# Retention and two feed-forward layers: q scaled inside its transposes, low parts of the early weights on GpSimd, and smaller conversion steps

## Chip, core and metric

One core of a Trainium2 chip runs the whole program. The metric is the device time of one execution in microseconds (us), the median over runs. The engines work from their own lists of instructions in order: TensorE (PE; its weight loads are PEld), VectorE (DVE), ScalarE (ACT), GpSimd (POOL) and SyncE (SP), which here only issues transfers. They wait for each other by semaphores.

## What is computed

Retention over four sequences of 576 tokens with 8 heads of 64, and behind it two feed-forward layers over the 2304 tokens:

```python
gamma = 1.0 - 2.0 ** (-5.0 - np.arange(H, dtype=np.float32))
rel = pos[:, None] - pos[None, :]
Dmat = np.where(rel >= 0, gamma[:, None, None] ** rel[None, :, :], 0.0)
attn = ((q @ k.T) / np.sqrt(64) * Dmat) @ v            # for each sequence and head
x = attn with its heads side by side                   # 2304 x 512
h = np.maximum(np.maximum(x @ w1, x @ w2), x @ w3)     # 2304 x 768
x2 = h @ w_out                                         # 2304 x 512
g = x2 @ w_gate
out = (g / (1 + np.exp(-g)) * (x2 @ w_val)) @ w_out2   # 2304 x 512, inner width 1536
```

The weights arrive in 64-bit form.

## The kernel before

**Units and visits.** The retention is cut into 32 units n: a sequence, a half of it (288 tokens, three chunks of 96) and a pair of heads. `visit(n)` loads unit n+4 (`a_load`), finishes unit n (`a_value`), computes the states and the scores of unit n+1 (`a_state`, `a_score`), prepares unit n+2 (`a_prep`), and between these does `slices` pieces of the first feed-forward layer (`f_slice`) and `convs` conversions of its weights. Visit 0 has neither, visits 1 and 2 one conversion, visits 3 to 7 one slice and one conversion, visits 8 to 12 five slices and three conversions. In visits 0 to 3 three products with zeros (`spin`) keep TensorE busy. Up to visit 12 every engine's order is the order of the code; from visit 13 only TensorE's is, and a scheduler sets the others.

**A unit's chain.** For units 0 to 15 `a_prep` transposes k and q on TensorE into PSUM (tp); ScalarE copies k's part (kt) and VectorE multiplies q's part by the decay g (qg). For units 16 to 31 VectorE transposes both. GpSimd scales k into ks. `a_state` multiplies ks and v into m_ps, VectorE adds that to the running state (st), and ScalarE spreads the state into stz. `a_score` multiplies kt and qg into s, and VectorE applies the decay mask (pT). `a_value` multiplies stz by qg and v by pT into o_ps; ScalarE makes the high part xh and VectorE the rest xl.

**A slice** is twelve products of a 128 x 128 piece of a weight's high or low part with xh or xl, into one of two PSUM buffers; ScalarE (first of three weights) or VectorE (the other two, hmax) empties it.

**A conversion** of one weight piece from 64 bits (`conv_steps`) is wz and wl on ScalarE, shift, or and add on VectorE, the high part (wh) on ScalarE and the low part (wlo) on the engine given, here VectorE. `win_phase` takes one step; `win_conv(i)` takes ScalarE's first step of weight i+1 beside the high part of weight i, then VectorE's step of i+1, then the low part of i. Weights 3, 4, 8, 9 and so on (i % 5 > 2) lie in tiles w64e, the others in w64; five are in flight.

**The later stages** (second matrix of the first layer, second layer) are not touched.

## Time and profile before

| | us |
|---|---|
| median of 3 runs | 886.98 (885.99 to 888.44) |
| the profiled execution | 885.56 |
| its span, first to last instruction | 883.8 |
| TensorE busy | 861.6 (97%) |
| VectorE busy | 411.4 (47%) |
| ScalarE busy | 278.9 (32%) |
| GpSimd busy | 140.8 (16%) |

The first value product of visit 1 starts at 16.82 us, of visit 8 at 53.77, of visit 13 at 109.89. These times cut the span into the stretches used below. In a row of the windows stand the stretch, its length, then for each engine its busy time and (xN) its instructions, then TensorE's granted clock as a share of 2.4 GHz, the busy share of the DMA engines and GB/s. In a row of the timeline stand start, duration, engine, line, operation, output<-inputs and, in brackets, the engine's idle time just before and what ended it. In rows by line and form stand count, busy us, mean ns and idle time before. A row of the chain has start, duration, engine, output, line and count.

### The profile page before, as it was taken

The page shows a single profiled execution, that of the slowest core. Times are in us where ns is not written, and L with a number is a line of the kernel's source. Part 1 is how long each engine was busy: PE and PEld are TensorE (multiplying, and loading weights), DVE is VectorE, ACT ScalarE, POOL GpSimd, SP SyncE. Part 2 cuts the span into 40 slices and gives each one's busy share as a digit, 9 for nine tenths or more (in the row PEclk, how much of TensorE's full clock was granted, in tenths as well). Part 3 has the DMA queues.
Part 4 walks back from the last instruction along what each step waited for, and adds up shares of the span by engine and source line. Part 5 has one row for each costly group of instructions (what it writes and reads, how often), then busy time and mean ns, then how long its engine had stood idle before and what let it go on. Part 6 is the DMA issues. An engine that isn't in the chain of part 4 may idle for free.

```text
span 883.8 us, 14602 instructions
## 1 busy us (share of the span) xinstructions
PE 861.6 (97%) x5924; PEld 754.9 (85%) x5924; DVE 411.4 (47%) x770; ACT 278.9 (32%) x576; POOL 140.8 (16%) x148
## 2 busy tenths in 40 slices
PE   8889999999999899999999999999999999999998
PEld 5678999999999899999888888888888888888886
DVE  3888844435333962112811642573383353323243
ACT  3656612111113741443732711341151131111111
POOL 2110000001000300543111111121111111111111
PEclk9999999999999999999999999999999999999999
DMA  8866765433201850331400300130030000000122
GB/s 212 196 183 171 215 135 101 92 82 76 60 28 50 258 164 28 92 97 55 143 1 0 120 24 1 48 96 1 1 122 21 1 1 1 1 0 1 48 90 77
DMA packets 128179, 68.34 MB, mean 77 GB/s; under 512 B 89488, under 2 KB 123408, under 8 KB 128112
## 3 DMA queue, kind: packets, MB, share of 16 engines
q1 hardware_dynamic: 127248, 66.78, 28.1%
q8 instruction: 46, 0.75, 0.3%
q10 hardware_dynamic: 864, 0.64, 0.3%
q14 instruction: 21, 0.17, 0.1%
HBM read 55.60 MB, written 11.80 MB: 76 GB/s over the span
## 4 chain that ended last, share of the span: by engine, by line
PE 81%; DMA 6%; DVE 5%; ACT 3%; issue 2%; POOL 1%; SPq 1%; POOLq 0%; DVEq 0%; ACTq 0%
PE ps L503 33%; PE ps L313 19%; PE ps L525 16%; PE ps L478 8%; DMA hf<-h_d 2%; PE s L213 2%; PE o_ps L254 1%; PE o_ps L257 1%; DMA h_d<-hmax 1%; DMA w<-in_moe_w_dram 1%; DVE wz L112 1%; DVE wl L113 1%; PE m_ps L229 1%; ACT wz L108 1%; POOL hl L453 1%
## 5 line engine op out<-in xcount | busy, mean ns | idle before, releaser
L313 PE MATMUL ps<-xl,wh 128*128 128x288 f32 x576 | 175.6, 305 | 8.0 <-DVE hmax L319 4.1
L503 PE MATMUL ps<-x2l,wrh 128*128 128x512 f32 (+1 forms) x480 | 179.4, 374 | 0.7 <-DVE sg L511 0.7
L503 PE MATMUL ps<-x2h,wrl 128*128 128x512 f32 (+1 forms) x480 | 179.2, 373 | 0.0
L503 PE MATMUL ps<-x2h,wrh 128*128 128x512 f32 (+1 forms) x480 | 179.1, 373 | 0.0
L313 PE MATMUL ps<-xh,wh 128*128 128x288 f32 x576 | 170.3, 296 | 0.0
L313 PE MATMUL ps<-xh,wlo 128*128 128x288 f32 x576 | 170.3, 296 | 0.0
L514 POOL TENSOR_TENSOR gl<-gf,gh 128x512 fp32r<-128x512 f32 (+1 forms) x60 | 75.2, 1253 | 388.8 <-ACT gh L513 388.8
L313 PEld LDWEIGHTS ps<-xl,wh 128*128 128x128 f32 x576 | 108.6, 189 | 14.2 <-DVE hmax L319 6.7
L511 DVE TENSOR_TENSOR sg<-ps,sg 128x512 f32<-128x512 f32 (+1 forms) x60 | 38.2, 636 | 170.8 <-ACT sg L510 170.7
L313 PEld LDWEIGHTS ps<-xh,wlo 128*128 128x128 f32 x576 | 108.9, 189 | 0.0
L313 PEld LDWEIGHTS ps<-xh,wh 128*128 128x128 f32 x576 | 108.8, 189 | 0.0
L503 PEld LDWEIGHTS ps<-x2l,wrh 128*128 128x128 f32 x480 | 90.4, 188 | 19.6 <-DVE sg L511 1.6
L503 PEld LDWEIGHTS ps<-x2h,wrl 128*128 128x128 f32 x480 | 90.4, 188 | 17.8
L503 PEld LDWEIGHTS ps<-x2h,wrh 128*128 128x128 f32 x480 | 90.5, 189 | 17.6
L525 PE MATMUL ps<-wrh,gl 128*128 128x512 f32 x216 | 85.8, 397 | 0.4 <-POOL gl L514 0.4
L525 PE MATMUL ps<-wrl,gh 128*128 128x512 f32 x216 | 85.6, 396 | 0.0
L510 ACT ACTIVATE sg<-ps 128x512 f32<-128x512 f32 (+1 forms) x60 | 33.2, 554 | 165.7 <-PE ps L503 165.7
L525 PE MATMUL ps<-wrh,gh 128*128 128x512 f32 x216 | 85.2, 394 | 0.0
L319 DVE TENSOR_TENSOR hmax<-ps,hmax 128x288 f32<-128x288 f32 x96 | 43.4, 453 | 84.4 <-PE ps L313 76.0
L513 ACT ACTIVATE gh<-gf 128x512 fp32r<-128x512 f32 (+1 forms) x60 | 35.2, 587 | 121.1 <-DVE gf L512 121.1
L512 DVE TENSOR_TENSOR gf<-ps,sg 128x512 f32<-128x512 f32 (+1 forms) x60 | 38.2, 636 | 65.4 <-PE ps L503 64.5
L531 DVE TENSOR_TENSOR acc<-ps,acc 128x512 f32<-128x512 f32 x90 | 61.8, 689 | 3.3 <-PE ps L525 2.7
(61 smaller groups left out, 1139.8 us busy)
## 6 DMA issues: line engine op xcount, KB each, us to landing
w<-in_moe_w_out_dram SPq DMA_DIRECT2D x18, 512.0 KB, 3.8
h_d<-hmax SPq DMA_DIRECT2D x48, 144.0 KB, 1.8
hf<-h_d SPq DMA_DIRECT2D x48, 144.0 KB, 2.3
w<-in_moe_w_dram SPq DMA_DIRECT2D x12, 512.0 KB, 4.6
w<-in_moe_w_gate_dram SPq DMA_DIRECT2D x12, 512.0 KB, 4.6
w<-in_moe_w_val_dram SPq DMA_DIRECT2D x12, 512.0 KB, 4.4
kn<-in_k_dram SPq DMA_DIRECT2D x64, 72.0 KB, 2.9
out_dram<-acc SPq DMA_DIRECT2D x18, 256.0 KB, 2.0
```

The lines of the kernel that those rows point to most:

```text
L213: pe.matmul(s[:, e, cs], u["kt"][hd, cs], u["qg"][hd, c], start=True, stop=True)
L313: pe.matmul(ps, l[:, ksl], r, start=n == 0, stop=n == 3 * KD - 1)
L319: dve.tensor_tensor(mx[hb], ps, mx[hb], ALU.max)
L478: pe.matmul(ps, l[:, es], r, start=n == 0, stop=n == 3 * F1 - 1)
L503: pe.matmul(ps[:, 0:tw], l[:, ksl], r, start=n == 0, stop=n == 3 * KD - 1)
L510: act.activation(sg[:, 0:tw], pr[0][:, 0:tw], ACTF.Sigmoid)
L511: dve.tensor_tensor(sg[:, 0:tw], pr[0][:, 0:tw], sg[:, 0:tw], ALU.mult)
L512: dve.tensor_tensor(gf[:, 0:tw], pr[1][:, 0:tw], sg[:, 0:tw], ALU.mult)
L513: act.activation(gh[:, 0:tw], gf[:, 0:tw], ACTF.Copy)
L514: pool.tensor_tensor(gl[:, 0:tw], gf[:, 0:tw], f(gh[:, 0:tw]), ALU.subtract)
L525: pe.matmul(ps, l[:, sl], r, start=n == 0, stop=n == 3 * GRP - 1)
L531: dve.tensor_tensor(a, ps, a, ALU.add)
```

## The change

- **q.** New constants q_t hold g to the power j for each head; GpSimd multiplies them once with the identity into eight diagonal tiles `dia` of 96 x 96. For units 0 to 15 q is no longer transposed: for each chunk and head, q (96 x 64) is the stationary operand and `dia` moves, so transposing and scaling are one product, six per unit in place of three transposes. ScalarE copies k's and q's part together (kq, 576 columns); VectorE's qg is gone there. For units 16 to 31 only buffers change (kq has 3, qt 1).
- **Low parts.** The 18 weights of the first layer have wlo on GpSimd.
- **Steps.** `conv_steps` stops in more places, and `conv_plan` takes, per weight i: shift and or of i, then wz of i+1; add of i, then wl of i+1; high part, then low part of i. The load of weight i+4 goes with the add of i.
- **Order.** xl of unit n now stands behind st of unit n+1 (`low`). For unit 0 the scores precede the states. `zero` is filled before the other tiles.
- **First loads.** cst_a and q0 go on ScalarE's queue, k0 and v0 on SyncE's, cst_g behind weight 1; weights 2 and 3 are loaded in visits 1 and 2.

```diff
+O_Q = O_E + NP
+O_G = O_Q + H
...
+            c[:CK, O_Q + 2 * pr + e] = g ** j
...
+    dia = att.tile([CK, H, CK], F32, name="dia", tag="dia", bufs=1)
...
         z = stg.tile([P, 512], U32, name="wz", tag="wz", bufs=2)
+        act.activation(f(z), f(u[:, :, 1]), ACTF.Copy, scale=float(2.0 ** -112))
+        yield
         l = stg.tile([P, 512], U32, name="wl", tag="wl", bufs=2)
-        act.activation(f(z), f(u[:, :, 1]), ACTF.Copy, scale=float(2.0 ** -112))
         act.activation(l, u[:, :, 0], ACTF.Copy, scale=float(2.0 ** -29))
         yield
         dve.tensor_scalar(z, z, 3, None, ALU.logical_shift_left)
         dve.scalar_tensor_tensor(z, u[:, :, 1], 0x80000000, z, ALU.bitwise_and, ALU.bitwise_or)
+        yield
         dve.tensor_tensor(l, z, l, ALU.add)
...
+    zero = att.tile([P, 512], BF16, name="zero", tag="zero", bufs=1)
+    pool.memset(zero, 0.0)
     stz = [att.tile([P, NC, 2, D], F32, name=f"stz{i}", tag=f"stz{i}", bufs=1) for i in range(3)]
...
-        kt = att.tile([P, C], F32, name="kt", tag="kt", bufs=2)
-        qg = att.tile([P, NC, CK], F32, name="qg", tag="qg", bufs=3)
+        kq = att.tile([P, 2, C], F32, name="kq", tag="kq", bufs=3)
+        kt, qg = kq[:, 0], kq[:, 1].rearrange("p (c m) -> p c m", c=NC)
...
-            for x, nm in ((0, "k"), (1, "q")):
-                for c in range(NC):
-                    pe.transpose(tp[:, x, c * CK:(c + 1) * CK],
-                                 u[nm][:, c].rearrange("p h d -> p (h d)"), ident)
-            act.activation(kt, tp[:, 0, 0:C], ACTF.Copy)
-            dve.tensor_tensor(qg, tp[:, 1, 0:C].rearrange("p (c m) -> p c m", c=NC), g, ALU.mult)
+            for c in range(NC):
+                pe.transpose(tp[:, 0, c * CK:(c + 1) * CK], u["k"][:, c].rearrange("p h d -> p (h d)"), ident)
+            for c in range(NC):
+                for e in range(2):
+                    pe.matmul(tp[64 * e:64 * e + 64, 1, c * CK:(c + 1) * CK], u["q"][:, c, e],
+                              dia[:, 2 * pr + e], start=True, stop=True)
+            act.activation(kq, tp[:, :, 0:C], ACTF.Copy)
         else:
-            qt = att.tile([P, C], F32, name="qt", tag="qt", bufs=2)
+            qt = att.tile([P, C], F32, name="qt", tag="qt", bufs=1)
...
-        dve.tensor_tensor(xl, o, f(xh), ALU.subtract)
         xs[(2 * b + h, pr)] = (xh, xl)
+        return lambda: dve.tensor_tensor(xl, o, f(xh), ALU.subtract)
...
-        win_step[i] = conv_steps(win_ld[i], hi, lo, dve)
+        win_step[i] = conv_steps(win_ld[i], hi, lo, pool)
...
             if phase == 3:
+                win_load(i + 4)
+            if phase == 5:
                 ready.add(i)
-    def win_conv(i, part=None):
-
-        for p, (j, ph) in enumerate(((i + 1, 0), (i, 2), (i + 1, 1), (i, 3))):
-            if part is None or p in part:
-                win_phase(j, ph)
-        if part is None or 3 in part:
-            win_load(i + 4)
+    wc = [0]
+
+    def conv_plan(convs):
+
+        for _ in range(convs):
+            i = wc[0]
+            if i < len(win_units):
+                wc[0] += 1
+                yield (i, 2), (i + 1, 0)
+                yield (i, 3), (i + 1, 1)
+                yield (i, 4), (i, 5)
...
-        a_value(n)
+        low = a_value(n)
...
         a_state(n + 1)
+        low()
         a_score(n + 1)
...
+        for j in range(slices + 1):
+            if j == min(2, slices - 1) or not slices:
                 a_prep(n + 2)
...
+            upto = -(-len(plan) * (j + 1) // (slices + 1))
+            for step in plan[done:upto]:
+                for i, ph in step:
+                    win_phase(i, ph)
+            done = upto
+            if j < slices:
+                f_some(1)
...
-    sp.dma_start(out=cst_a, in_=consts[:, 0:O_G])
-    a_load(0, "kq")
-    act.dma_start(out=cst_g, in_=consts[:, O_G:O_D])
-    a_load(0, "v", act)
+    act.dma_start(out=cst_a, in_=consts[:, 0:O_G])
+    a_load(0, "k")
+    a_load(0, "q", act)
+    a_load(0, "v")
+    pool.tensor_tensor(dia, ident.unsqueeze(1).to_broadcast([CK, H, CK]),
+                       q_t.unsqueeze(2).to_broadcast([CK, H, CK]), ALU.mult)
     act.dma_start(out=cst_d, in_=consts[0:CK, O_D:NCONST])
...
     win_load(1)
-    win_load(2)
-    win_load(3)
+    sp.dma_start(out=cst_g, in_=consts[:, O_G:O_D])
     spin(8)
     a_prep(0)
     spin(3)
+    a_score(0)
     a_state(0)
-    a_score(0)
...
+        if 1 <= n < 3:
+            win_load(n + 1)
```

VectorE, one visit's worth of work around visit 5, before. wz, wl and wlo are a weight's parts, w64e its 64-bit form:

```order
L195 TENSOR_TENSOR qg<-tp,cst_g 128x288
L111 TENSOR_SCALAR wz<-wz 128x512
L112 SCALAR_TENSOR_TENSOR wz<-w64e,wz 128x512
L113 ISA wl<-wz,wl 128x1024
L319 TENSOR_TENSOR hmax<-ps,hmax 128x288
L117 TENSOR_TENSOR wlo<-wl,wh 128x512
L261 TENSOR_TENSOR xl<-o_ps,xh 128x288
L239 SCALAR_TENSOR_TENSOR st<-st,cst_a,m_ps 128x64 x2
L215 TENSOR_TENSOR pT<-s,cst_d 96x576
```

And the same with the change:

```order
L116 TENSOR_SCALAR wz<-wz 128x512
L117 SCALAR_TENSOR_TENSOR wz<-w64e,wz 128x512
L119 ISA wl<-wz,wl 128x1024
L334 TENSOR_TENSOR hmax<-ps,hmax 128x288
L248 SCALAR_TENSOR_TENSOR st<-st,cst_a,m_ps 128x64 x2
L271 TENSOR_TENSOR xl<-o_ps,xh 128x288
L224 TENSOR_TENSOR pT<-s,cst_d 96x576
```

qg and wlo are gone, and st stands ahead of xl.

ScalarE, from the end of unit 8 on (visit 8), before:

```order
L260 ACTIVATE xh<-o_ps 128x288
L243 ACTIVATE stz_83<-st 64x3x64 x2
L108 ACTIVATE wz<-w64e 128x512
L109 ACTIVATE wl<-w64e 128x512
L115 ACTIVATE wh<-wl 128x512
L317 ACTIVATE hmax<-ps 128x288
L194 ACTIVATE kt<-tp 128x288
```

And with the change:

```order
L269 ACTIVATE xh<-o_ps 128x288
L252 ACTIVATE stz_86<-st 64x3x64 x2
L111 ACTIVATE wz<-w64e 128x512
L114 ACTIVATE wl<-w64e 128x512
L332 ACTIVATE hmax<-ps 128x288
L121 ACTIVATE wh<-wl 128x512
L204 ACTIVATE kq<-tp 128x576
```

hmax stands ahead of wh, and the copy of k's part has become the copy of both.

TensorE, the retention part of visit 6, before:

```order
L254 MATMUL o_ps<-qg,stz_83 64x96 x6
L257 MATMUL o_ps<-pT,vn 64x96 x6
L229 MATMUL m_ps<-vn,ks 64x64 x4
L213 MATMUL s<-qg,kt 96x96 x6
L192 MATMUL tp<-cst_a,kn 128x96 x3
L192 MATMUL tp<-cst_a,qn 128x96 x3
```

And with the change:

```order
L263 MATMUL o_ps<-kq,stz_86 64x96 x6
L266 MATMUL o_ps<-pT,vn 64x96 x6
L238 MATMUL m_ps<-vn,ks 64x64 x4
L222 MATMUL s<-kq 96x96 x6
L199 MATMUL tp<-cst_a,kn 128x96 x3
L202 MATMUL tp<-dia,qn 64x96 x6
```

The three transposes of q have become six products in the same place.

## Rows read from the trace of the kernel before

**Rows 1.** Windows: stretch, length, PE, PEld, DVE, ACT, POOL busy, clock, DMA share, GB/s.

```profile
16.82:53.77 36.95, 31.71 (x420) 26.31 (x419) 30.89 (x64) 21.91 (x53) 5.45 (x8) 1.00 0.85 209
...
53.77:109.89 56.12, 52.16 (x510) 49.05 (x510) 48.95 (x96) 34.12 (x71) 3.94 (x6) 0.97 0.70 191
...
60.00:65.00 5.00, 3.01 (x15) 2.90 (x16) 4.21 (x8) 3.94 (x8) 0.82 (x1) 0.79 0.50 133
65.00:70.00 5.00, 4.50 (x39) 4.10 (x39) 4.03 (x8) 2.11 (x5) 0.00 (x0) 0.87 0.44 134
...
109.89:140.00 30.11, 29.38 (x302) 27.77 (x302) 13.83 (x34) 5.96 (x18) 2.83 (x4) 1.00 0.67 134
```

**Rows 2.** Waits of TensorE to 110 us: total, times, longest.

```profile
PE o_ps L254 <- ACT stz L243: 3.6, 5, 1.5
PE ps L313 <- ACT hmax L317: 2.5, 2, 2.0
PE psz L337 <- POOL zero L332: 2.4, 1, 2.4
...
PE tp L192 <- DMA kn<-in_k_dram: 1.4, 2, 1.2
PE tp L192 <- DMA qn<-in_q_dram: 1.0, 1, 1.0
```

**Rows 3.** Timeline of VectorE from one qg to the next; TensorE's m_ps of visit 5.

```profile
37.50 0.46 DVE L195 TENSOR_TENSOR qg<-tp,cst_g 128x288 f32<-128x288 f32 x1 [0.58 <-ACT kt L194]
...
40.49 0.68 DVE L117 TENSOR_TENSOR wlo<-wl,wh 128x512 fp32r<-128x512 f32 x1
...
41.45 0.59 DVE L239 SCALAR_TENSOR_TENSOR st<-st,cst_a,m_ps 128x64 f32<-128x64 f32 x2
41.95 0.75 DVE L215 TENSOR_TENSOR pT<-s,cst_d 96x576 f32<-96x576 f32 x1
43.29 0.46 DVE L195 TENSOR_TENSOR qg<-tp,cst_g 128x288 f32<-128x288 f32 x1 [0.58 <-ACT kt L194]
...
38.08 0.44 PE L229 MATMUL m_ps<-vn,ks 96*64 96x64 f32 x6
```

**Rows 4.** Timeline of ScalarE and TensorE in visit 8.

```profile
59.14 0.73 ACT L243 ACTIVATE stz<-st 64x192 f32<-64x192 f32 x2 [2.55 <-DVE st L239]
...
61.54 0.39 ACT L317 ACTIVATE hmax<-ps 128x288 f32<-128x288 f32 x1
...
61.99 0.40 PE L313 MATMUL ps<-xl,wh 128*128 128x288 f32 x1 [2.00 <-ACT hmax L317]
```

**Rows 5.** Groups by line and form: GpSimd's and ScalarE's prices.

```profile
L514 POOL TENSOR_TENSOR gl<-gf,gh 128x512 fp32r<-128x512 f32 x48 | 64.4, 1343 | 325.9 <-ACT gh L513 325.9
...
L184 POOL TENSOR_TENSOR ks<-kn,cst_a 96x384 f32<-96x384 f32 x16 | 13.6, 852 | 114.1 <-PE m_ps L229 66.9 <-DMA kn<-in_k_dram 47.2
...
L510 ACT ACTIVATE sg<-ps 128x512 f32<-128x512 f32 x48 | 28.7, 599 | 153.5 <-PE ps L503 153.5
```

**Rows 6.** The chain that ended last, early: products of the retention part.

```profile
12.65 0.50 PE tp L192 x6
...
14.06 0.50 PE o_ps L257 x12
...
14.91 0.68 PE s L213 x12
```

**Rows 7.** GpSimd beside VectorE: timeline, and means by form, 12 to 130 us.

```profile
41.72 0.82 POOL L184 TENSOR_TENSOR ks<-kn,cst_a 96x384 f32<-96x384 f32 x1 [3.54 <-DMA kn<-in_k_dram]
...
61.02 0.82 POOL L184 TENSOR_TENSOR ks<-kn,cst_a 96x384 f32<-96x384 f32 x1 [3.33 <-DMA kn<-in_k_dram]
61.05 1.34 DVE L112 SCALAR_TENSOR_TENSOR wz<-w64e,wz 128x512 uint32<-128x512 uint32 x1
...
L215 DVE TENSOR_TENSOR pT<-s,cst_d 96x576 f32<-96x576 f32 x16 | 12.0, 747 | 0.3 <-PE s L213 0.3
...
L112 DVE SCALAR_TENSOR_TENSOR wz<-w,wz 128x512 uint32<-128x512 uint32 x16 | 11.0, 690 | 0.4
```

More of the change, by code (lines that the diff above doesn't have):

```diff
@@ L39 @@
 O_E = O_KS + NP * 2
-O_G = O_E + NP
+O_Q = O_E + NP
+O_G = O_Q + H
 O_D = O_G + NP * CK
@@ L87, in retention_moe @@
     ks_t = cst_a[0:CK, O_KS:O_E].rearrange("p (r e) -> p r e", r=NP)
-    e_t = cst_a[:, O_E:O_G]
+    e_t = cst_a[:, O_E:O_Q]
+    q_t = cst_a[0:CK, O_Q:O_G]
     g_t = cst_g.rearrange("p (r m) -> p r m", r=NP)
     d_t = cst_d.rearrange("p (r e m) -> p r e m", r=NP, e=2)
+    dia = att.tile([CK, H, CK], F32, name="dia", tag="dia", bufs=1)
     def load_w(src, early=False):
@@ L328, in f_some @@
                 f_slice(*fq.pop(0))
-    zero = att.tile([P, 512], BF16, name="zero", tag="zero", bufs=1)
-    pool.memset(zero, 0.0)
     def spin(n):
@@ L339, in visit @@
     def visit(n, slices, convs):
-        nonlocal wc
         a_load(n + 4)
-        a_value(n)
+        low = a_value(n)
         if n == 2 * NP - 1:
@@ L353, in visit @@
         a_state(n + 1)
+        low()
         a_score(n + 1)
-        plan = [p for _ in range(convs) for p in ((0, 1), (2,), (3,))]
+        plan = list(conv_plan(convs))
         done = 0
-        def some(upto):
-            nonlocal done, wc
-            while done < min(upto, len(plan)):
-                if wc < len(win_units):
-                    win_conv(wc, plan[done])
-                if 3 in plan[done]:
-                    wc += 1
-                done += 1
-        for j in range(slices):
-            if j == 2 or slices < 3 and j == 0:
-                a_prep(n + 2)
-            some(-(-len(plan) * (j + 1) // (slices + 1)))
-            f_some(1)
-        if not slices:
-            a_prep(n + 2)
-        some(len(plan))
-    wc = 0
+        for j in range(slices + 1):
+            if j == min(2, slices - 1) or not slices:
+                a_prep(n + 2)
+            upto = -(-len(plan) * (j + 1) // (slices + 1))
[5 more added lines that the diff above has]
+                f_some(1)
     START = 13
```

## The prediction

> **What bounds the kernel now.** I began with the windows, one row per stretch between visits' first value matmuls. From 140 us on TensorE is the bound: already from 109.89 to 140 it is busy 29.38 of 30.11 us [rows 1]. Its list of instructions hardly changes, so what it waits for early is what can be won, and what is added to it is what can be lost. From 16.82 us (visit 1) to 53.77 (visit 8) it is busy 31.71 of 36.95 us: 5.24 lost. From 53.77 to 109.89 (visits 8 to 12) it is busy 52.16 of 56.12: 3.96 lost. After that 0.73 more is lost by 140.
>
> Then the waits: up to 110 us TensorE waited mostly for ScalarE's stz (3.6), for ScalarE's hmax (2.5) and for two loads of k (1.4) [rows 2]. ScalarE is not the cause. In the timeline of visits 4 and 5, VectorE's rows from one qg to the next show one gap, 0.58 us, before qg itself, which waits for ScalarE's kt [rows 3]. The last products m_ps of visit 5 start on TensorE at 38.08 and take 0.44, and VectorE takes up the st that reads them at 41.45: it runs 2.9 us late. stz follows st, and the next visit starts with stz. At 59.14 ScalarE starts an stz for which it had stood 2.55 us behind VectorE; hmax, four instructions later in its order, starts at 61.54, and that ends TensorE's longest wait, 2.0 us [rows 2, 4].
>
> That hole costs twice. After it the granted clock is 0.79 in 60 to 65 us and 0.87 in 65 to 70 [rows 1], which is time at the lower of two levels (1.2 GHz, 0.5): (0.21 + 0.13) x 5 = 1.70 us is lost by it.
>
> So up to 110 us the chain goes through VectorE: 30.89 us busy of 36.95, then 48.95 of 56.12.
>
> **The change, part by part.** *qg leaves VectorE in units 0 to 15.* One qg is 0.46 us [rows 3]; its place is taken by ScalarE, whose copy grows from 288 to 576 columns. 512 columns out of PSUM take 0.60 [rows 5]; scaled, 0.67 for 576. ScalarE is busy 21.91 and 34.12 us of the two stretches, so the growth lies in its free time, and kq is read a visit later. If that cover fails, stz waits behind it, some 0.3 us a visit.
>
> *The low part leaves VectorE*: 18 x 0.68 [rows 3]. On GpSimd 512 columns of the same operation take 1.34 in the last stage, 384 of ks 0.85 [rows 5]: I take 1.34, the same form. GpSimd is busy 5.45 of 36.95 us, so it has room; TensorE uses a weight a visit later or more. ks stands behind the low part in GpSimd's order and is wanted a visit later.
>
> *VectorE's sum.* Visits 1 to 7: 30.89 - 7 x 0.46 - 7 x 0.68 = 22.9 us. Visits 8 to 12, with the 11 remaining weights: 48.95 - 5 x 0.46 - 11 x 0.68 = 39.2. TensorE's own work is 31.71 and 52.16. So TensorE is last in both stretches, unless GpSimd takes it back (below). st also goes ahead of xl, which helps stz; and shift and or now come a step after ScalarE's wz, so their wait for it goes.
>
> *The q products, on TensorE.* Three transposes become six products per unit. The row of six transposes is 0.50, so q's three are 0.25. The products have 96 rows, 64 columns of weights and 96 columns moving, and write two halves in turn: that is the form of the second part of a_value, 0.50 for its six. The scores, six too, take 0.68 [rows 6]. So a unit gains 0.25 us (ends: 0, if a product cost what half a transpose costs, and 0.43). I take 0.25, the same form. Seven fall into visits 1 to 7: 1.75. Five into visits 8 to 12: 1.25. One later.
>
> *The start.* TensorE waits 2.4 us for zero, 0.2 of the 1.4 for the first k, and 1.0 for q0 [rows 2]. zero is now filled first, cst_a and cst_g leave the path of k0, and q0 goes on ScalarE's queue. All of it gone is 1.2 (what zero gains only brings the spins forward). Against it: the diagonal tiles (768 columns, twice the 0.85 of ks, so 1.7) go ahead of q0's products and of the first ks on GpSimd, and the first products run at the lower clock. Between -1.2 and +1.5; I take -0.3, since the diagonal needs only cst_a, which is now ScalarE's first load.
>
> *The queues.* Weights 2 and 3 and cst_g no longer stand ahead of unit 4's loads on SyncE's queue, for whose k TensorE waited 1.2. Weight 3 now goes behind weight 4. Nothing else passes anything that it must wait for.
>
> *The sum.* Visits 1 to 7: -5.24 of waits + 1.75 of products, and 0.9 for waits that stay (a sixth, for bunching), gives -2.6. Visits 8 to 12: -3.96 - 1.70 of clock + 1.25 + 1.6 that stay (weights come there three a visit, so more bunches), gives -2.8. Later: -0.73 + 0.25 + 0.28, -0.2. Start: -0.3. Together -5.9. The profiled execution took 885.56 us (span 883.8), so 879.7; it stands 1.42 below the median of the runs, 886.98, so **881.1**.
>
> **What speaks against it.** At 61.02 GpSimd starts a ks of 0.82 us, and the VectorE instruction of 61.05 takes 1.34 us, where the same operation on the other staging tiles takes 0.69: as if it had begun only at 61.70, just before GpSimd ended. At 41.72 a ks overlaps pT, which reads its products from PSUM, and pT takes 0.75, the mean of its 16 rows [rows 3, 7]. The Trainium skill has this as a rule (SBUF — State Buffer, section "Who interferes with whom"): VectorE instructions with two SBUF inputs, or in a mode that uses two ports, and GpSimd instructions that read SBUF shut each other out for the whole of an instruction. Both pairs of rows agree with it. By that rule the low part, put on GpSimd, is not off VectorE at all; what that gives is the first rival.
>
> **The rivals.**
> (A) *GpSimd's low parts hold VectorE up* (slower). Each low part of 1.34 us falls on shift, or or add. VectorE then has 22.9 + 7 x 1.34 = 32.3 and 39.2 + 11 x 1.34 = 53.9 us; with the holes that it has today (6.06 and 7.17) the stretches take 38.4 and 61.1, against 36.95 and 56.12: +6.4, and 885.56 - 0.3 + 6.4 + 1.42 = 893. It decides from about 1.0 us lost per low part, the 0.68 saved plus qg's share (12 x 0.46 / 18 = 0.31). For it: the row at 61.05. Against: the low part comes after hi, which comes after the add of the same weight; VectorE's next work is then hmax, st, xl and pT, all with an operand in PSUM, as pT at 41.95. With three weights a visit it will hit sometimes; that is in the 1.6.
> (B) *Loads pace visits 1 to 7* (no difference). One visit moves 432 KB of k, q, v and one weight of 512 KB, near 0.97 MB; at the 209 GB/s of the stretch [rows 1] that is 4.6 us. Visits shortened to 34.4/7 = 4.9 leave almost nothing. If loads pace, the first stretch gains nothing and the late weights take half of the second: 885.56 - 1.4 + 1.42 = 885.6. Against: DMA is busy 0.85 there, so it has some reserve.
> (C) *The wait moves to ScalarE* (no difference). hmax stays in order behind two steps of conversion and now kq; if TensorE's buffers wait for it as at 61.54, the clock falls again, and the second stretch only loses products: 885.56 - 2.6 - 0.3 + 1.25 + 1.42 = 885.3. Against: ScalarE is busy 34.12 of 56.12 us there [rows 1].
>
> **How the numbers follow.** Forecast 0.72, A 0.08, B 0.12, C 0.08. 0.3% (2.7 us) is about what a measurement of this kernel can tell from no change; so faster ends at 884.3. The forecast's own range goes from all waits gone with the start at its best, 885.56 - 1.2 - 5.24 - 5.66 - 0.73 + 3.25 + 1.42 = 877.4, a little lower for cheaper products, to the scores' price (13 x 0.18 = 2.3) and more bunching, some 884.5. I set 876.5 to 886.5: B and C are in, A is out. Faster 0.70 (0.02 of the forecast's cases are too small), same 0.20 (B, C), slower 0.10 (A, and a dear start).
>
> **What would show it.** Right: from visit 1 to visit 8 some 34.4 us in place of 36.95, from visit 8 to visit 13 some 53.3 in place of 56.12, no stretch at the lower clock after 15 us, stz started by st soon after m_ps, six q products in about 0.50. Wrong: VectorE's shift, or and add longer than 0.45 and 0.70 beside GpSimd's low part (A); waits of wz or ks for their loads, with DMA over 1.0 (B); waits of TensorE for ScalarE's hmax (C); q products near 0.68.

## The result, and the profile after

The changed kernel takes **879.09 us** (876.93 to 880.24, 4 runs) against 886.54 of before beside it; the ratio is 0.9906 (95% interval 0.9887 to 0.9925), so 0.9% faster. Run again it took 878.36 (876.77 to 881.25, 6 runs; 0.9903, 0.9882 to 0.9923). Forecast were 881.1 us and a range of 876.5 to 886.5. The profiled execution took 880.24 us, span 878.4; against the span of before, 883.8, it is 5.4 shorter, where the sum of the prediction had 5.9. That this agrees is partly luck, as the stretches show (starts of visits as in [rows 1]):

| stretch | before | after | difference | forecast |
|---|---|---|---|---|
| to visit 0 / to visit 1 | 13.51 / 16.82 | 10.67 / 14.47 | -2.84 / -2.35 | -0.3 |
| visit 1 to visit 8 | 36.95 | 33.92 | -3.03 | -2.6 |
| visit 8 to visit 13 | 56.12 | 51.43 | -4.69 | -2.8 |
| visit 13 to the end | 773.91 | 778.58 | +4.67 | -0.2 |

The windows of the changed kernel (columns as in [rows 1]) answer to the first two rows of that group. TensorE is busy 33.48 of 33.92 us and then 51.43 of 51.43; VectorE has gone from 30.89 to 24.69 and from 48.95 to 44.20. Then two stretches with a lower clock stand where before had 1.00:

```profile
14.47:48.39 33.92, 33.48 (x483) 27.76 (x482) 24.69 (x51) 25.19 (x56) 13.42 (x13) 1.00 0.89 225
48.39:99.82 51.43, 51.43 (x557) 48.72 (x557) 44.20 (x75) 32.67 (x66) 22.48 (x18) 1.00 0.74 206
100.00:105.00 5.00, 3.49 (x23) 3.31 (x20) 3.35 (x6) 1.50 (x3) 0.91 (x1) 0.72 0.80 136
105.00:110.00 5.00, 5.00 (x53) 4.50 (x51) 1.47 (x4) 0.82 (x2) 0.00 (x0) 0.94 0.57 125
280.00:300.00 20.00, 18.04 (x120) 17.47 (x121) 18.15 (x32) 14.43 (x28) 6.68 (x7) 0.91 0.84 248
```

TensorE's waits over the whole span (total, times, longest) answer to [rows 2]. The 3.6 us for stz, the 1.4 for k and the 1.0 for q are no longer among them; what is left for hmax waits mostly for VectorE, and late (at 102 and 289 us). The wait for k isn't gone for good: in the second profile (from the run again) TensorE waits 1.4 us for k, and visits 1 to 7 take 34.87 us in place of 33.92.

```profile
PE ps L328 <- DVE hmax L334: 3.4, 2, 1.9
...
...
PE ps L328 <- ACT hmax L332: 0.8, 1, 0.8
```

The timeline shows where both waits for VectorE's hmax stand. On VectorE an add that belongs to w_out, which the scheduler put in early, takes 1.31 us beside a ks of GpSimd; hmax comes behind it, and TensorE has stood 1.51 us. The second hole is at 288.74, again in front of hmax.

```profile
100.10 0.91 POOL L192 TENSOR_TENSOR ks<-kn,cst_a 96x384 f32<-96x384 f32 x1 [1.88 <-PE tp L202]
100.25 1.31 DVE L119 CUSTOM_DVE_ANT_0 wl<-wz,wl 128x1024 uint16<-128x1024 uint16 x1
101.49 0.44 DVE L334 TENSOR_TENSOR hmax<-ps,hmax 128x288 f32<-128x288 f32 x1
...
101.99 0.43 PE L328 MATMUL ps<-xl,wh 128*128 128x288 f32 x1 [1.51 <-DVE hmax L334]
...
288.74 0.40 PE L328 MATMUL ps<-xl,wh 128*128 128x288 f32 x1 [1.86 <-DVE hmax L334]
```

The holes are 1.51 and 1.86 us; the clock costs (0.28 + 0.06) x 5 = 1.7 and 0.09 x 20 = 1.8. The holes alone are not what is new. From visit 13 on all waits of TensorE come to 7.0 us, in before to 5.4; between 270 and 340 us it is idle for 2.95 in the one and 3.03 in the other. So of the 4.67 us in the table's last row some 1.5 are waits and some 3.5 the lower clock, which before has nowhere in that stretch (1.00). The second profile of the same kernel has both holes too (1.57 and 1.94), with the clock at 1.00 behind the first and 0.91 around the second.

What GpSimd's low part, and the ks that now runs behind it, do to VectorE is seen in groups by line up to 110 us (busy, mean ns). On GpSimd the low part takes 1355 ns, as priced. On VectorE the add takes 830 (747 before), shift 596 (424), or 773 [rows 7: 690]:

```profile
L119 DVE CUSTOM_DVE_ANT_0 wl<-wz,wl 128x1024 uint16<-128x1024 uint16 x20 | 16.5, 830 | 2.2
L116 DVE TENSOR_SCALAR wz<-wz 128x512 uint32<-128x512 uint32 x22 | 13.1, 596 | 1.4 <-ACT wz L111 1.4
L117 DVE SCALAR_TENSOR_TENSOR wz<-w,wz 128x512 uint32<-128x512 uint32 x16 | 12.4, 773 | 0.5
...
L123 POOL TENSOR_TENSOR wlo<-wl,wh 128x512 fp32r<-128x512 f32 x18 | 24.4, 1355 | 47.6 <-ACT wh L121 47.6
```

With or on the tiles w64e (1037 after, 848 before, 6 of them) the growth is 20 x 0.083 + 22 x 0.172 + 16 x 0.083 + 6 x 0.189 = 7.9 us, 0.44 per low part. The timeline shows on which instructions it falls. St and xl, which read PSUM, keep their 0.60 (two) and 0.45 beside a low part; a shift that meets one takes 1.04 in place of 0.42, as if it began near the end of the low part (96.24). The low part can be held up as well: the one at 66.11, with an or that began at 66.10, takes 1.84 in place of 1.29, and the add behind that or takes 1.57 in place of 0.69. Of the 18 low parts ten meet only work that reads PSUM, among them all six that fall into visits 1 to 7; eight meet a shift, an or or an add.

```profile
66.10 0.69 DVE L117 SCALAR_TENSOR_TENSOR wz<-w,wz 128x512 uint32<-128x512 uint32 x1
66.11 1.84 POOL L123 TENSOR_TENSOR wlo<-wl,wh 128x512 fp32r<-128x512 f32 x1 [3.34 <-ACT wh L121]
...
66.93 1.57 DVE L119 CUSTOM_DVE_ANT_0 wl<-wz,wl 128x1024 uint16<-128x1024 uint16 x1
...
85.02 1.29 POOL L123 TENSOR_TENSOR wlo<-wl,wh 128x512 fp32r<-128x512 f32 x1 [2.58 <-ACT wh L121]
85.39 0.60 DVE L248 SCALAR_TENSOR_TENSOR st<-st,cst_a,m_ps 128x64 f32<-128x64 f32 x2 [0.74 <-ACT st L246]
85.90 0.45 DVE L271 TENSOR_TENSOR xl<-o_ps,xh 128x288 fp32r<-128x288 f32 x1
...
94.96 1.28 POOL L123 TENSOR_TENSOR wlo<-wl,wh 128x512 fp32r<-128x512 f32 x1 [2.58 <-ACT wh L121]
...
95.48 1.04 DVE L116 TENSOR_SCALAR wz<-wz 128x512 uint32<-128x512 uint32 x1 [0.29 <-ACT wz L111]
```

### The profile page after: what moved, and what is told of

Read it like the earlier page. It is cut to its first block, busy times and chain, and to the rows that moved or that the text cites. A ratio compares the mean times of both kernels' runs of the same rounds, so it can differ in the third digit from the quotient of the medians.

```text
span 878.4 us, 14871 instructions
## 1 busy us (share of the span) xinstructions
PE 865.7 (99%) x6068; PEld 759.3 (86%) x6068; DVE 401.3 (46%) x736; ACT 282.8 (32%) x576; POOL 167.8 (19%) x167
## 4 chain that ended last, share of the span: by engine, by line
PE 86%; DMA 5%; DVE 3%; ACT 2%; issue 2%; POOL 1%; SPq 1%; ACTq 0%; POOLq 0%; DVEq 0%
PE ps L510 33%; PE ps L328 22%; PE ps L532 16%; PE ps L485 7%; DMA hf<-h_d 2%; PE s L222 2%; PE o_ps L263 2%; PE o_ps L266 1%; POOL hl L460 1%; PE m_ps L238 1%; DMA w<-in_moe_w_dram 1%; PE tp L202 1%; DVE wz L117 1%; SPq L161 1%; DVE wz L116 1%
## 5 line engine op out<-in xcount | busy, mean ns | idle before, releaser
L460 POOL TENSOR_TENSOR hl<-hf,hh 128x288 fp32r<-128x288 f32 x48 | 39.4, 840 | 127.8 <-ACT hh L459 126.9
```

The lines of the kernel that those rows point to most:

```text
L460: pool.tensor_tensor(hl, hf, f(hh), ALU.subtract)
```

## The experiments

Medians and ratios are each against before run beside it (886.7, 888.0 and 886.9 us in the three sets).

| kernel | us | ratio, 95% interval |
|---|---|---|
| changed kernel, and again | 879.09, 878.36 | 0.9906 (0.9887-0.9925), 0.9903 (0.9882-0.9923) |
| e1 old loads | 882.19 | 0.9945 (0.9925-0.9965) |
| e2 zero late | 883.00 | 0.9957 (0.9939-0.9976) |
| e14 zero late, two spins | 878.21 | 0.9900 (0.9878-0.9923) |
| e3 low part on VectorE | 882.06 | 0.9948 (0.9928-0.9969) |
| e5 old steps | 888.37 | 1.0013 (0.9999-1.0026) |
| e13 old steps, low part on VectorE | 883.84 | 0.9965 (0.9950-0.9979) |
| e7 before, low part on GpSimd | 892.42 | 1.0062 (1.0040-1.0084) |
| e4 q transposed | 880.01 | 0.9926 (0.9908-0.9944) |
| e9 hmax first | 880.33 | 0.9921 (0.9903-0.9938) |
| e8 order to 16 | 881.40 | 0.9927 (0.9901-0.9953) |
| e12 w_out late | 879.88 | 0.9919 (0.9900-0.9938) |

**The low part and the steps: e3, e7, e5, e13.** My theory was that VectorE had been relieved by the low part; the rival was A, that GpSimd takes it back. In e3 only the engine goes back:

```diff
-        win_step[i] = conv_steps(win_ld[i], hi, lo, pool)
+        win_step[i] = conv_steps(win_ld[i], hi, lo, dve)
```

> The changed kernel with the 18 low parts on VectorE again, all else as it is. They took 0.685 us each there and 1.355 on GpSimd, beside which shift, or and add on VectorE were longer by 7.9 us in all, 0.44 per low part. Theory: VectorE only gets 0.685 - 0.44 = 0.25 us per weight more to do, 1.7 in visits 0 to 7 where it is busy 24.69 of 33.92 us and 2.7 in visits 8 to 12; it stays below TensorE, so +0 to +1.5 us, 879.1 to 880.6, with single holes in visits 8 to 12 where three weights fall into a visit. The working of the prediction instead gave the low part the larger share of the relief of VectorE (18 x 0.68 = 12.2 us): by that, holes and a lower clock come back in visits 8 to 12 and it takes 882 to 884. Rival A (low parts on GpSimd hold VectorE up as much as they save): 878 to 879, shift and add back at 0.42 and 0.75 us.

It took 882.06, 3 to 3.7 us more than the changed kernel and more than I expected from VectorE's sum; the time that the prediction's working gave was nearer. The trace puts only part of that on the low part. The add is back at 705 ns, the low part costs 692 each, and visits 1 to 12 take 1.7 us more. The largest single loss comes behind them: a hole of 3.16 us in front of hmax at 109.76, with the clock at 0.86, 0.50 and 0.96 from 105 to 120 us (3.4 us). There VectorE isn't busy; it has stood 4.30 us for a load of q (108.88), and hmax stands behind the transpose of that q. Whether that hole belongs to the low part, by the order that the scheduler then chooses, or to this execution is not shown. First its groups by line up to 110 us, then its timeline:

```profile
L119 DVE CUSTOM_DVE_ANT_0 wl<-wz,wl 128x1024 uint16<-128x1024 uint16 x20 | 14.0, 705 | 0.6
L123 DVE TENSOR_TENSOR wlo<-wl,wh 128x512 fp32r<-128x512 f32 x18 | 12.4, 692 | 10.1 <-ACT wh L121 10.1
```

```profile
108.88 0.48 DVE L208 STREAM_TRANSPOSE qt<-qk 128x288 f32<-128x288 f32 x1 [4.30 <-DMA qk<-in_q_dram]
...
109.76 0.61 PE L328 MATMUL ps<-xl,wh 128*128 128x288 f32 x1 [3.16 <-DVE hmax L334]
```

e7 is the opposite: before, with the same edit the other way round (dve to pool).

> The kernel before with one edit: the 18 low parts go to GpSimd. Steps, q, loads and zero stay as before. Theory (VectorE sets the end up to 110 us): VectorE loses 18 x 0.68 = 12.2 us and gets some 18 x 0.44 = 7.9 back beside GpSimd, so 4 us of it are free; ks behind the low part is no risk. The holes of 1 to 2 us in visits 1 to 12 shrink by a third: 883 to 885 in place of 886.6. If the low part alone were worth what the prediction's working gave it (7 x 0.68 + 5 x 0.68 of waits and 1.7 of clock), 879 to 882. Rival A (GpSimd holds VectorE up as much as it saves): 886 to 888.

My theory fell: 892.42, slower than before. Here rival A is what happens. The add takes 1364 ns (747 before): 20 x 0.62 = 12.3 us on it alone, as much as the 18 x 0.685 saved, and shift and or grow as well. TensorE's wait for VectorE's hmax is 10.0 us over the span. The group by line up to 115 us, then the wait:

```profile
L113 DVE CUSTOM_DVE_ANT_0 wl<-wz,wl 128x1024 uint16<-128x1024 uint16 x20 | 27.3, 1364 | 2.5
```

```profile
PE ps L313 <- DVE hmax L319: 10.0, 10, 1.7
```

So the low part on GpSimd takes 3.0 to 3.7 us off in one kernel and adds 4.5 in the other. What differs is the rest of the change: the steps, q, the order, the loads. I formed a new theory, that the small steps are what keeps the low part off VectorE's way, and tried the changed kernel with the old steps on either engine (e5; e13 also has dve as in e3):

```diff
         act.activation(f(z), f(u[:, :, 1]), ACTF.Copy, scale=float(2.0 ** -112))
-        yield
...
         act.activation(l, u[:, :, 0], ACTF.Copy, scale=float(2.0 ** -29))
         yield
...
         dve.scalar_tensor_tensor(z, u[:, :, 1], 0x80000000, z, ALU.bitwise_and, ALU.bitwise_or)
-        yield
         dve.tensor_tensor(l, z, l, ALU.add)
...
-                yield (i, 2), (i + 1, 0)
-                yield (i, 3), (i + 1, 1)
-                yield (i, 4), (i, 5)
+                yield (i + 1, 0), (i, 2)
+                yield (i + 1, 1),
+                yield (i, 3),
```

> The changed kernel with the steps of conversion as before (wz and wl in one step, shift, or and add in the next, then hi, then the low part), the low part still on GpSimd. In the kernel before with the low part on GpSimd the add beside it grew from 747 to 1364 ns and the kernel got 4 to 6 us slower. Theory: with the old steps the add of the next weight always stands where the low part of the last one runs, VectorE waits some 0.6 us per weight more, and TensorE waits for hmax and stz again: add near 1.3 us, 884 to 889. Rival: the q products have freed VectorE of 0.46 us per unit, so that there is room for it: 878 to 881 as the changed kernel (878.4 to 879.1).

> The same with the low part on VectorE too: of the change only the q products, the order of xl and the first loads are left. With small steps the low part on VectorE cost 3.4 us (882.1 against 878.7). Theory: the steps matter only through GpSimd, so on VectorE old and small steps are within 1.5 us: 881 to 883.5, add back near 0.75 us. The low part on GpSimd then is worth 3.4 us with small steps and less than nothing with old ones. Rival: the small steps are worth as much by themselves (their wait for wz goes from VectorE): 885 or more.

888.37 is as the theory said; 883.84 is just above its 881 to 883.5 and below the rival's 885. The four cells:

| | low part on GpSimd | on VectorE |
|---|---|---|
| small steps | 879.09 / 878.36 | 882.06 |
| old steps | 888.37 | 883.84 |

By time the steps can't be told apart on VectorE (the intervals of e3 and e13 overlap); on GpSimd they are worth 9 to 10 us. By the traces, one profile of each and two of the changed kernel, visits 1 to 11 take 79.3 and 80.2 us in the changed kernel, 81.0 in e3, 91.9 in e5 and 85.5 in e13: there small steps are worth 4.5 us on VectorE too, which e3 loses again in the hole at 109.76. In that stretch the low part on GpSimd saves 0.7 to 1.7 us with small steps and costs 6.4 with old ones. The timeline of e5 shows why. Its hi (wh) ends at 61.41 + 0.63 = 62.04, and the low part starts at 62.11, just when or ends (61.43 + 0.69 = 62.12); the add after it takes 1.70, where it takes 0.69 alone (66.75), as if it had begun at 63.27, near the end of the low part at 63.40. Below are that piece of e5's timeline, and the add's group up to 110 us in e5 and in e13:

```profile
61.41 0.63 ACT L119 ACTIVATE wh<-wl 128x512 fp32r<-128x512 f32 x1
61.43 0.69 DVE L116 SCALAR_TENSOR_TENSOR wz<-w64e,wz 128x512 uint32<-128x512 uint32 x1
...
62.11 1.29 POOL L121 TENSOR_TENSOR wlo<-wl,wh 128x512 fp32r<-128x512 f32 x1 [4.07 <-DVE wz L116]
...
62.26 1.70 DVE L117 CUSTOM_DVE_ANT_0 wl<-wz,wl 128x1024 uint16<-128x1024 uint16 x1
...
66.75 0.69 DVE L117 CUSTOM_DVE_ANT_0 wl<-wz,wl 128x1024 uint16<-128x1024 uint16 x1
```

```profile
L117 DVE CUSTOM_DVE_ANT_0 wl<-wz,wl 128x1024 uint16<-128x1024 uint16 x20 | 28.8, 1438 | 2.6
```

```profile
L117 DVE CUSTOM_DVE_ANT_0 wl<-wz,wl 128x1024 uint16<-128x1024 uint16 x20 | 14.2, 712 | 2.7 <-ACT wl L113 0.2
```

With the old plan hi of one weight stands behind wz and wl of the next on ScalarE, so it ends while VectorE is at that next weight's or, and the low part runs into the add: for 15 of the 18 low parts the add takes 1.55 to 1.70. With the new plan hi and the low part follow the add, and VectorE goes on to hmax, st, xl and pT. The Trainium skill (SBUF — State Buffer, section "Who interferes with whom") says that the one that issues first holds the other off for its whole length, and that a VectorE instruction with at most one input in SBUF, outside the two-port modes, does not meet GpSimd at all. These rows agree with the first, in both directions (62.26; 66.11 above), and st and xl beside a low part (85.39 and 85.90 above) with the second. The shift at 95.48 has one input in SBUF and was held up all the same; it fits only if it ran in one of those modes, which no row here shows.

**The start: e1, e2, e14.** e1 puts the first loads back and also fills zero behind the stz tiles, as in before; e2 does the latter alone. The edit of e1:

```diff
-    zero = att.tile([P, 512], BF16, name="zero", tag="zero", bufs=1)
-    pool.memset(zero, 0.0)
     stz = [att.tile([P, NC, 2, D], F32, name=f"stz{i}", tag=f"stz{i}", bufs=1) for i in range(3)]
     for t in stz:
         pool.memset(t, 0.0)
+    zero = att.tile([P, 512], BF16, name="zero", tag="zero", bufs=1)
+    pool.memset(zero, 0.0)
...
-    act.dma_start(out=cst_a, in_=consts[:, 0:O_G])
-    a_load(0, "k")
-    a_load(0, "q", act)
-    a_load(0, "v")
+    sp.dma_start(out=cst_a, in_=consts[:, 0:O_G])
+    a_load(0, "kq")
+    act.dma_start(out=cst_g, in_=consts[:, O_G:O_D])
+    a_load(0, "v", act)
...
-    sp.dma_start(out=cst_g, in_=consts[:, O_G:O_D])
+    win_load(2)
+    win_load(3)
```

> The changed kernel with the first loads as they stood before: cst_a first on the queue of SyncE and k0 and q0 behind it, cst_g and v0 on that of ScalarE, weights 2 and 3 early, zero filled after the three stz tiles. The diagonal tiles, q products, low part on GpSimd and the small steps stay. Theory: the 2.84 us that visit 0 starts earlier (10.67 in place of 13.51) come from the loads and from zero, by spins that begin at 1.31 instead of 2.38 and first transposes that do not stand for k0, so that the clock is up before the first scores. Then visit 0 starts at 13 to 13.6 us here and the kernel takes 881.5 to 882 in place of 879.1. Rival: the gain comes from q products that need no cst_g and from kq in one copy; then visit 0 starts by 11.5 and the time stays within 1 us of that of the changed kernel. If loads also paced visits 1 to 7 (weights 2 and 3 stand ahead of k4 again), TensorE waits for k4 and visit 1 to visit 8 takes over 35 us in place of 33.92.

Between theory and rival: visit 0 starts at 12.29, so 1.62 of the 2.84 us go with the loads and zero together. q0 comes late again (TensorE's timeline, first row), and 882.19 is some 3 us above the changed kernel, more than the start alone explains; of the rest 0.4 stands in visits 1 to 7 (34.32 us) and the remainder behind visit 13.

```profile
7.32 0.86 PE L202 MATMUL tp<-dia,qn 96*64 96x96 f32 x12 [1.40 <-DMA qn<-in_q_dram]
...
12.29 0.55 PE L263 MATMUL o_ps<-kq,stz 128*64 128x96 f32 x8
```

The other 1.2 us are gained in e1 too. TensorE's timeline of before, then of the changed kernel:

```profile
10.65 1.25 PE L213 MATMUL s<-qg,kt 64*96 64x96 f32 x12
11.83 0.82 PE L337 MATMUL psz<-zero 128*128 128x512 bf16 x3
```

```profile
1.31 3.60 PE L350 MATMUL psz<-zero 128*128 128x512 bf16 x8 [1.31 <-POOL zero L142]
4.70 0.69 PE L199 MATMUL tp<-cst_a,kn 96*128 96x96 f32 x3
5.32 1.23 PE L202 MATMUL tp<-dia,qn 96*64 96x96 f32 x12
...
7.30 0.75 PE L222 MATMUL s<-kq 64*96 64x96 f32 x12
...
9.14 0.41 PE L199 MATMUL tp<-cst_a,kn 96*128 96x96 f32 x3
9.48 0.72 PE L202 MATMUL tp<-dia,qn 96*64 96x96 f32 x12
...
10.67 0.55 PE L263 MATMUL o_ps<-kq,stz 128*64 128x96 f32 x8
```

The granted clock of the windows is 1.00 from 0 to 15 us in both kernels, so the level is read here from durations: the same instructions take close to twice as long before some moment as after it. The first k transposes and q products of the changed kernel are still on the slow side (0.69 and part of 1.23; 0.41 and 0.72 for the second unit), but its scores take 0.75 where before's take 1.25: the change of level comes some five us sooner, and the spins, m_ps and scores of the start are shorter by it. What brought it sooner stays open: e1 has the loads and the zero of before, with its first spin at 2.38 as there, and its first k transposes already take 0.41 at 5.50.

> The changed kernel with one line moved: zero is filled after the three stz tiles, as before. Theory: the spins of TensorE then begin near 2.4 us in place of 1.31, everything up to the first k transposes (4.70) is shorter by as much of spinning, and since k0 sets the transposes the loss is only what the clock does: if it rises at 7.5 instead of 6.5 us, half of that us is lost, +0.5 to +0.6, so 879.6. Rival: the whole shift of 1.07 us of zero reaches visit 0, because the eight spins are a fixed number and end that much later: visit 0 at 11.7, 880.2. Second rival: nothing changes (879.1), the spins only fill a wait.

Neither: visit 0 starts at 10.58, as early as in the changed kernel, yet 883.00. The trace shows one hole at 28 to 31 us: a spin waits for ScalarE's hmax, which stands behind wz, which waits for a weight; in the windows the clock is low for the next ten us, (0.27 + 0.42) x 5 = 3.4 us more.

```profile
29.46 0.66 ACT L111 ACTIVATE wz<-w64e 128x512 f32<-128x512 f32 x1 [2.23 <-DMA w64e<-in_moe_w_dram]
...
30.56 0.40 ACT L332 ACTIVATE hmax<-ps 128x288 f32<-128x288 f32 x1
...
31.02 0.38 PE L350 MATMUL psz<-zero 128*128 128x512 bf16 x1 [2.97 <-ACT hmax L332]
```

```profile
30.00:35.00 5.00, 3.98 (x50) 3.17 (x51) 1.63 (x5) 2.61 (x7) 1.84 (x2) 0.73 1.18 245
35.00:40.00 5.00, 5.00 (x44) 4.50 (x46) 2.23 (x5) 2.40 (x4) 1.37 (x2) 0.58 0.87 217
```

In the changed kernel wz waits even longer there (2.80 us, to 29.96) and hmax starts at 31.10, with no hole. The order of the instructions is the same; the semaphore of the third spin of visit 3 is not (first e2, then the changed kernel):

```
L350 MATMUL psz<-zero 128x512 [waits Activation_49]
L350 MATMUL psz<-zero 128x512 [waits PE_49]
```

Of the two PSUM buffers that spins and slices share, e2's third spin got the one that hmax reads. So the run says nothing of zero. e14 is e2 without that spin, `spin(3 if n < 3 else 2)`:

> Zero late once more, with two spins behind the slice of visit 3 in place of three. In zero late the third of them got the PSUM buffer that hmax reads (it waits for ScalarE), in the changed kernel the other one (it waits for TensorE alone): a wait of 2.97 us and the lower clock after it, which is not zero's doing. Theory: without that third spin zero late shows no hole at 28 to 31 us, visit 0 starts at 10.6 us as before, and the kernel takes 877.5 to 880, as the changed one (878.4 to 879.1): zero is worth nothing. Rival: zero's 1.07 us does come back after visit 0 by the clock; then 880.5 to 883 without any wait of a spin for ScalarE.

878.21 and no such hole: zero's place is worth nothing that can be measured in the time, and e2's 4 us went with one filler instruction on the buffer that hmax reads. (What of the 1.07 reaches visit 0 can't be told: it starts at 11.22 in e14 and at 10.58 in e2, whose instructions are the same up to there, and the eight profiles with zero early and the q products lie between 10.18 and 10.80.) Before that, the changed kernel had been run again, to see whether such runs were its own too:

> The changed kernel as it is, once more, beside others on one chip. Its first four runs lie at 876.9 to 880.2 us; the kernel with zero late, whose visit 0 starts as early (10.58 us), has ten runs from 879.3 to 885.6, and its profiled run of 885.0 shows one hole of 2.97 us at 28 to 31 us, ScalarE standing 2.23 us for the load of a weight (wz) with hmax behind it. Theory: that wait is a matter of when the load lands, so the changed kernel itself has such runs: a spread of 4 us and more here, median 880 to 883. Rival: zero late is dearer by 3 to 4 us by a way that its profile does not show; then the changed kernel stays at 877 to 880.5 here too.

Nearer the rival: the median is 878.36. The spread of over 4 us is there (876.8 to 881.3), the slow median is not.

**The q products: e4.** q is transposed by the identity and scaled by qg on VectorE again:

```diff
-                for e in range(2):
-                    pe.matmul(tp[64 * e:64 * e + 64, 1, c * CK:(c + 1) * CK], u["q"][:, c, e],
-                              dia[:, 2 * pr + e], start=True, stop=True)
-            act.activation(kq, tp[:, :, 0:C], ACTF.Copy)
+                pe.transpose(tp[:, 1, c * CK:(c + 1) * CK], u["q"][:, c].rearrange("p h d -> p (h d)"), ident)
+            act.activation(kt, tp[:, 0, 0:C], ACTF.Copy)
+            dve.tensor_tensor(qg, tp[:, 1, 0:C].rearrange("p (c m) -> p c m", c=NC), g, ALU.mult)
```

> The changed kernel with q transposed by the identity and scaled by qg on VectorE again; no diagonal tiles, cst_g on the queue of ScalarE behind q0. Low part on GpSimd, small steps and the other loads stay. Theory: TensorE loses 0.3 us of work per unit (tp 0.89 to 0.59), VectorE gets 0.46 per unit. In visits 1 to 7 TensorE is busy 33.48 of 33.92 us and VectorE 24.69, so the 7 x 0.46 = 3.2 fit; then the q products were a pure cost of about 12 x 0.3 = 3.6 us and this kernel takes 875.5 to 877. Rival: the order of VectorE matters, not its share: qg stands ahead of st, stz comes late, holes of 1 to 2 us with the clock down after them return in visits 8 to 12, and it takes 880 to 883.

880.01, at the lower end of the rival's range and, by the intervals, not to be told from the changed kernel. Its windows:

```profile
13.21:46.74 33.53, 30.60 (x421) 25.55 (x420) 24.85 (x56) 22.34 (x53) 11.80 (x13) 1.00 1.01 235
46.74:101.29 54.55, 51.60 (x511) 48.74 (x511) 46.51 (x82) 32.86 (x68) 22.83 (x19) 0.97 0.71 193
...
60.00:65.00 5.00, 5.00 (x60) 4.56 (x60) 2.82 (x6) 2.96 (x7) 1.73 (x2) 0.71 0.88 264
```

In visits 1 to 7 TensorE has 2.88 us less to do and gains 0.39, but not evenly. e4 starts visit 1 at 13.21, 1.26 us before the changed kernel; then, with DMA at 1.01, it waits for k and xl (1.0 us each), and visit 4 starts at 28.32, against 28.39. So in visits 1 to 3 rival B's pace is real, and products saved there win nothing. Visits 4 to 7 take 18.42 us against 20.00: there the products cost 0.40 us a visit. In visits 8 to 12, qg brings back holes in front of VectorE's hmax (2.9 us in three, the longest 2.1) and a lower clock behind them: 54.55 us against 51.43.

**The places that are left: e9, e8, e12.** e9 puts ScalarE's wz and wl behind hmax in visits 1 to 7:

```diff
-                yield (i, 2), (i + 1, 0)
-                yield (i, 3), (i + 1, 1)
-                yield (i, 4), (i, 5)
+                if convs == 1:
+                    yield (i, 2), (i, 3)
+                    yield (i, 4), (i, 5), (i + 1, 0), (i + 1, 1)
+                else:
+                    ...
```

> The changed kernel with one order changed in visits 1 to 7, where one weight is converted per visit: ScalarE's wz and wl of the next weight come behind hmax and hi, not ahead of them. Theory: in some runs of the changed kernel ScalarE stands for a load at wz while hmax waits behind it, TensorE waits 1 to 3 us for hmax, and the clock is low for the next 5 to 10 us (in zero late: 0.73 and 0.58 in 30 to 40 us). With hmax first the spread shrinks and the slow end goes: 876.5 to 880, a median 1.5 to 3 us below the changed kernel of the same call. Rival: the wait only moves, since xh and stz of the next visit then stand behind wz: same spread and median within 1 us.

The spread is smaller (879.9 to 881.3), the median is not: 880.33. TensorE now waits for xl at the start of visit 8 (0.28) and for VectorE's hmax within it, and visit 8 takes 12.88 us (11.41 in the changed kernel):

```profile
60.20 0.40 PE L332 MATMUL ps<-xl,wh 128*128 128x288 f32 x1 [0.86 <-DVE hmax L338]
```

e8 (`START = 16` in place of 13) was to keep w_out's steps out of visits 13 to 15.

> The changed kernel with the hand-written order of all engines kept to visit 15 in place of visit 12, so that w_out conversions cannot be placed ahead of hmax on VectorE in visits 13 to 15. Theory: the hole of 1.51 us at 102 us (TensorE waits for hmax, VectorE has two adds of a w_out weight ahead of it) and the lower clock of 100 to 110 us (0.72 and 0.94, 1.7 us) go: visit 13 to visit 14 takes some 17 in place of 20.0 us, and the time is 2 to 3 us below that of the changed kernel of the same call. Rival: the later stages lose what is won, since w_out conversions come later and the next stage waits for them: no difference.

It did not do that: instructions written later are still placed between hand-ordered ones, and the hole is there unchanged (1.76 us at 102.15, this time with the clock at 1.00 behind it). 881.40; where its extra 2 to 3 us come from was not settled, save that they come late: visit 14 starts at 118.48, against 119.33 in the second profile of the changed kernel. e12 holds the loads themselves back, by a product of visit 17 that GpSimd writes into each staging tile ahead of its load:

```diff
+        if behind is not None:
+            xh, xl = behind
+            pool.tensor_tensor(t.bitcast(F32)[:, 0:C], f(xh), f(xl), ALU.mult)
...
         visit(n, 5, 0)
+        if n == 17:
+            b, h, pr = units[n]
+            for i in range(3):
+                c2_load(i, behind=xs[(2 * b + h, pr)])
```

> The changed kernel with the first three loads of w_out held back to visit 17: GpSimd writes a product of that visit's xh and xl into the staging tile ahead of each load, so that the scheduler cannot place shift, or and add of w_out among visits 10 to 13. Theory: in the changed kernel those steps, with ks on GpSimd beside them (or 1.20, add 1.31 us), stand ahead of hmax at 100 to 101.5 us and make the hole of 1.5 us before visit 13, with up to 1.7 us of lower clock behind it. Without them hmax is in time, visit 13 starts some 18 us before visit 14 rather than 20, and the time is 1.5 to 3 us below that of the changed kernel: 875.5 to 877.5. Rival: the same steps come at 150 us or at 275 us, where hmax stands behind them as well (there is a hole of 1.9 us at 289 us already): 878 to 880.

The rival: the hole at 102 us is gone and visit 14 starts at 116.27 in place of 119.85, but the steps stand ahead of hmax again where they come now (1.72 us at 158.19). From 270 to 340 us TensorE is idle for 3.85 us, without the edit for 2.95; but the clock there is 1.00 in place of 0.98, which makes up for it. So what uses up the 3.6 us won by visit 14 is only in part shown. E12's timeline and window, then the window of the changed kernel:

```profile
158.19 0.40 PE L331 MATMUL ps<-xl,wh 128*128 128x288 f32 x1 [1.72 <-DVE hmax L337]
```

```profile
270.00:340.00 70.00, 66.15 (x509) 63.88 (x504) 44.00 (x82) 32.67 (x65) 8.48 (x9) 1.00 0.52 153
```

```profile
270.00:340.00 70.00, 67.05 (x522) 65.27 (x523) 44.49 (x83) 32.10 (x64) 8.77 (x9) 0.98 0.50 153
```

879.88, no better than the changed kernel. None of the others beats it by more than the intervals tell.

## Why the prediction was right, point by point

- **What bounded before**: right. VectorE's lateness made the waits for stz and hmax. With 24.69 and 44.20 us busy it no longer does, and TensorE is busy throughout.
- **The start** (-0.3): mis-sized. -2.84 to visit 0, -2.35 to visit 1, which is what the sum needs. Its best end was -1.2, the waits alone; that the products behind them would run at the upper level of the clock had no term, nor had the q products of the first three units (visit 0 takes 3.80 in place of 3.31). 1.62 us go with the loads and zero (e1). zero, which I counted as bringing the spins forward only, is worth nothing in the time (e14): right.
- **Visits 1 to 7** (-2.6): -3.03. Of the 0.9 us for waits that stay 0.44 is there.
- **Visits 8 to 12** (-2.8): -4.69. The 1.6 us for bunching was too much: there is no hole in that stretch. The bunch came behind it, in visit 12, where I had put nothing.
- **The q products** (+0.25 a unit, ends 0 and 0.43): +0.30 in visit 12 up to visit 13's first products, where nothing waits in either kernel (6.06 us against 5.76); 0.40 in visits 4 to 7 against e4. Inside the bounds, nearer the scores' price than I took: from start to start the row of six takes 0.55 (at 99.27) to 0.65 (at 9.48), not 0.50.
- **The low part** (1.34 us on GpSimd, 0.68 off VectorE): its own time was right (1355 ns). VectorE's relief was 0.685 - 0.44 = 0.24 each, not 0.68: the sum for VectorE (22.9 and 39.2) came out 1.8 and 5.0 higher. It didn't matter, since TensorE's own work stayed above both.
- **The small steps**: the step that failed in weight. The prediction gave them one clause (shift and or no longer wait for wz). The clause was right: VectorE's idle time in front of shift, for wz, is 1.4 us up to 110 us, 6.0 in before and 12.6 in e13. What it left out is where they put hi, and with it the low part. With the low part on GpSimd they are worth 9 to 10 us, and without them the change as a whole gains nothing (e5).
- **Rival A** was put at 0.08 and at 893. Its deciding point, 1.0 us lost per low part, was not reached (0.44). The argument against it, that VectorE's next work reads PSUM, holds with the small steps alone, and there for ten of the 18. Where it doesn't (e7), the growth is 20 x 0.62 + 22 x 0.13 + 16 x 0.06 = 16.2 us, 0.90 per low part against 0.68 saved, and the kernel takes 892.4.
- **Rival B**: hidden but real in visits 1 to 3, which the loads pace in e4; visits 5 to 7 of e4 take 4.62, 4.31 and 4.63, under TensorE's 4.87 to 5.00 in the changed kernel. **Rival C**: did not come; 0.8 us for ScalarE's hmax.
- **After visit 13** (-0.2): +4.67 in the profiled execution, some 1.5 of it waits and 3.5 clock. It set off what the start and the visits gained beyond the forecast: that the sum came out is luck in this. The forecast took the later stages as unchanged, but the scheduler fills what VectorE has free with w_out's steps, ahead of hmax. e12 shows that these steps make the hole at 102 us. The lower clock behind it is in one of the two profiles only, so the 1.7 us are not the hole's price in every run; why it fell in one and not in the other stays open. What makes the second hole, and the clock of 0.91 around it, was not tried.

## What to carry to other kernels

Before moving a step from VectorE to GpSimd, look at which VectorE instructions will stand beside it in its order: beside those that read PSUM the moved step cost them nothing here, beside back-to-back steps in SBUF it cost as much as it saved or more. Here where the steps were cut decided the sign, so parts of a change are to be tried together as well as alone: from e13, GpSimd alone cost 4.5 us, the small steps alone gained under 2 (not told apart from nothing, with e3's hole in it), both together 4.7 to 5.5. A hole that a variant shows is to be followed to what ended it before its time is put down to the edit: e3's was a load. When a variant is slower than its edit explains, compare what each instruction waits for, not only the order: one filler product on another buffer went with 4 us.

## What the runs showed of the hardware

- VectorE and GpSimd held each other up in both directions: in the changed kernel a low part that starts 0.01 us behind an or takes 1.84 us against 1.29, and the add behind that or takes 1.57 against 0.69 (66.10 to 66.93). St and xl, with an operand in PSUM, were not held up (0.60 for two, 0.45).
- One filler product that waits 2.97 us costs as much again by the clock: 0.73 and 0.58 in the next ten us. Behind holes of 1.5 to 1.8 us at one and the same place the granted clock was 0.72 in one profile of the changed kernel and 1.00 in the other and in e8.
- By the durations of TensorE's rows (the granted clock of the windows is 1.00 there) the level rose between 5 and 6.5 us in the changed kernel, in e1 and in e2 (k's first transposes take 0.41 at 5.50 and 5.40 there), whether the spins began at 1.31 or at 2.38; in before the first row wholly at the upper level is that of 11.83, and TensorE had waited 1.00 us for q0 at 7.86 [rows 2]. e2 and e14 have the same instructions up to there, and the same transposes take 0.41 in one and 0.69 in the other: the moment differs from one execution to the next.
